# Attention feeding a gated MLP on one core: two heads' float32 scores in the two 64-row halves of the array, v loaded in the order of the keys, and the products of p and v in one group

## The chip, the core and the metric

The kernel runs on 1 core of one Trainium2 chip. The metric is the device time of one execution in microseconds (us). Before the change the median of 3 runs is 748.91 us (748.83 to 749.66).

## What is computed

The reference is rotary attention over 4 batches x 8 heads x 576 positions x 64, and then an MLP with a sigmoid gate over the 2304 resulting rows of 512:

```python
q_rot, k_rot = (rotate(q), rotate(k))
scores = scale * np.matmul(q_rot, k_rot.transpose(0, 1, 3, 2))
scores = scores - np.max(scores, axis=-1, keepdims=True)
attn = np.exp(scores)
attn = attn / (np.sum(attn, axis=-1, keepdims=True) + 1e-09)
attn_out = np.matmul(attn, v)                      # [4, 8, 576, 64]
x = attn_out.transpose(0, 2, 1, 3).reshape(2304, 512)
h = x @ w_in                                       # [2304, 2048]
g = h * (1.0 / (1.0 + np.exp(-1.702 * h)))
out = (g @ w_out).astype(np.float32)               # [2304, 512]
```

## The kernel before

The 32 heads are worked as 16 pairs of heads, pair n from batch n // 4. For each pair `prep` loads q and k, turns them by the rotary angles (three elementwise operations on `RAW` and `BT`, VectorE or GpSimd), transposes them on TensorE (line 455, into `PT`) and copies them out of PSUM. `attention` then makes nine tiles of scores of 128 queries x 576 keys (four per head, and tile 4 with the last 64 queries of both heads), each into one of two PSUM buffers `SPS`. VectorE copies a tile out with its sign turned and finds the extreme of each row (line 602), ScalarE takes the exponential and the sum (line 605), giving `PP` (`PJ` for tile 4). The tiles are transposed on TensorE into `PT`, copied to SBUF, and multiplied with v into `AV`; the result goes to `XS`, is divided by the sums, split into a high and a low part and written to `x_dram`.

There are two ways to full float32 precision. The first pairs use plain float32 matmuls, which TensorE runs in two passes. For the first three pairs (`n_plain_qk=3`) the rotated k and q of one head lie in rows 0 to 63 of a buffer `KP` whose rows 64 to 127 are zero (a GpSimd memset, line 521), one buffer per head, and a score tile is a matmul over all 128 rows, one head at a time (line 585). For the first eight (`n_plain_av=8`) p and v are plain float32 too: `weighted_both` handles the query tiles 0 and 1, then 2 and 3, of both heads, one 128-key step at a time: transpose (line 740) into `PT`, copy into one of two buffers `PW`, and the two heads' matmuls into the two halves of 64 output columns of the array (line 755), with a last matmul over both heads' remaining keys (line 751). `weighted_last` does the same for tile 4 (lines 773 and 789). All other pairs split numbers into a high and a low part in the type fp32r and use more, cheaper matmuls: scores at line 596 from `KA`, `KB`, `QT`, `QZ` (filled by lines 348, 350 and 497, and a DMA that moves 64 rows, line 505), p and v at lines 645 and 673.

The MLP (`moe`) works in 9 chunks of 256 rows of x. For each of 16 column blocks it does 12 matmuls of 256 columns with `win` into `PT` (line 908), a gate (lines 914 and 916, result `T`, split into `G`), and 6 matmuls of 512 columns with `wout` into the second `SPS` buffer (line 925). Its weights are themselves split into high and low parts on the chip (`weight`, lines 858 to 877, buffers `OW`, `CW`, `O`, `CV`). A chunk can start when all pairs of its batch have written their part of `x_dram`; for the fourth pair (n=3) the first 256 rows are written ahead of the rest (`halved0=3`).

The order of all instructions is made when the program is built. Each operation carries a priority (`PLANNED`, `PREP_AT`, `PAIR_AT`, `PAIR_LEN`, `MOE_AT`, `WEIGHT_AT` ...), `Plan.run` plays the operations through once with assumed durations, picks the engine for those that may run on two ("ACT DVE": the first named unless it is later by a wait), and the instructions are issued in the order of the start times that come out. Each engine then works through its own list strictly in order.

## Time and profile before

| | |
|---|---|
| median of the runs | 748.91 us (748.83 to 749.66) |
| span of the profiled execution, first to last instruction | 746.6 us |
| what lies around the span (median less span; the profiled execution's own time is not listed apart) | 2.3 us |
| TensorE (PE) busy | 720.2 us, 96% |
| VectorE (DVE) busy | 496.6 us, 67% |
| ScalarE (ACT) busy | 427.6 us, 57% |
| GpSimd (POOL) busy | 262.1 us, 35% |

Busy time of TensorE is modelled: a float32 matmul shows as two records, one a pass, and each record lasts longer than the distance to the next, because matmuls are pipelined. What a run of matmuls costs is therefore read from the start of its first to the start of what follows. A row of the timeline merges such a run and shows its start, its length, and the number of records.

### The profile page before, as it was taken

The numbers are of one execution on the slowest core, as the hardware profiler recorded it, in microseconds if no ns is written. First come the engines' busy times: TensorE is split into PE (matmuls) and PEld (weight loads), VectorE is DVE, ScalarE is ACT, GpSimd is POOL, SyncE is SP. The second block draws the span as 40 slices with busy tenths as digits, with TensorE's granted clock in tenths as the row PEclk, the third lists the DMA queues.
The fourth block names the chain that finished last, engine by engine and source line by source line (L and its number), as shares of the span: only waits on it lengthen the run. The fifth ranks groups of instructions, "written<-read, shape, count | busy, mean of one in ns | idle before, by whom it ended". The sixth has DMA issues, their size and how long they took to land.

```text
span 746.6 us, 14127 instructions
## 1 busy us (share of the span) xinstructions
PE 720.2 (96%) x4921; PEld 622.3 (83%) x4921; DVE 496.6 (67%) x1188; ACT 427.6 (57%) x1047; POOL 262.1 (35%) x295
## 2 busy tenths in 40 slices
PE   6898979999999999999999999999999999999997
PEld 5565647787777899999999989999999999999896
DVE  5899999788898887467787787877752222322222
ACT  3778778577876764366677666766643232222322
POOL 6566757465554544044343627121110000000000
PEclk8999999999999999999999999999999999999999
DMA  5545477656445653222232343421003020100000
GB/s 133 154 148 129 137 198 196 169 153 178 146 129 159 192 164 104 92 72 60 71 87 74 87 126 102 127 75 35 32 19 115 1 85 0 57 29 1 29 1 29
DMA packets 103911, 72.75 MB, mean 97 GB/s; under 512 B 67856, under 2 KB 88352, under 8 KB 103840
## 3 DMA queue, kind: packets, MB, share of 16 engines
q1 hardware_dynamic: 103840, 71.85, 34.4%
q8 instruction: 39, 0.64, 0.3%
q14 instruction: 32, 0.26, 0.1%
HBM read 48.87 MB, written 15.28 MB: 86 GB/s over the span
## 4 chain that ended last, share of the span: by engine, by line
PE 78%; DVE 11%; ACT 4%; issue 2%; DMA 2%; SPq 1%; POOL 0%; ACTq 0%; DVEq 0%; POOLq 0%
PE PT L908 26%; PE SPS L925 25%; PE SPS L596 8%; PE AV L673 5%; PE PT L645 5%; PE AV L755 3%; PE PT L740 2%; ACT PP L605 1%; DVE PP L602 1%; PE PT L455 1%; DVE RAW L353 1%; DVE QT L497 1%; DMA RAW<-in_q_dram 1%; PE SPS L585 1%; DVE CW L871 1%
## 5 line engine op out<-in xcount | busy, mean ns | idle before, releaser
L908 PE MATMUL PT<-XC,win 128*128 128x256 f32 x1728 | 244.2, 285 | 0.2 <-DVE T L916 0.2
L908 PEld LDWEIGHTS PT<-XC,win 128*128 128x128 f32 x1728 | 227.2, 189 | 11.9 <-DVE T L916 1.5
L925 PE MATMUL SPS<-wout,G 128*128 128x512 f32 x864 | 234.3, 400 | 0.3 <-ACT G L340 0.3
L925 PEld LDWEIGHTS SPS<-wout,G 128*128 128x128 f32 x864 | 150.4, 189 | 25.3 <-issue 0.8
L916 DVE SCALAR_TENSOR_TENSOR T<-T,PT 128x256 f32<-128x256 f32 x144 | 60.2, 418 | 93.2 <-ACT T L914 92.1
L605 ACT ACTIVATE PP<-PP,ST 128x576 f32<-128x576 f32 x128 | 99.3, 776 | 32.2 <-DVE PP L602 31.4
L914 ACT ACTIVATE T<-PT 128x256 f32<-128x256 f32 x144 | 55.1, 383 | 105.4 <-PE PT L908 103.3
L602 DVE TENSOR_SCALAR_CACHE_REDUCE PP<-SPS 128x576 f32<-128x576 f32 x128 | 95.5, 752 | 21.9 <-PE SPS L596 13.9
L353 DVE TENSOR_TENSOR G<-T,G 128x256 fp32r<-128x256 f32 x120 | 54.0, 450 | 62.0 <-ACT G L340 55.0
L340 ACT CAST G<-T 128x256 fp32r<-128x256 f32 x121 | 49.0, 405 | 67.2 <-PE SPS L925 65.4
L344 POOL TENSOR_SCALAR G<-T 128x256 fp32r<-128x256 f32 x23 | 9.6, 417 | 203.7 <-PE SPS L925 149.2
L662 DVE TENSOR_TENSOR PH<-PT,PH 128x512 fp32r<-128x512 f32 (+4 forms) x128 | 65.5, 528 | 18.0 <-ACT PH L340 16.1
L340 ACT CAST PH<-PT 128x384 fp32r<-128x384 f32 (+4 forms) x113 | 49.7, 453 | 36.7 <-PE PT L645 31.0
L673 PE MATMUL AV<-PH,VS 128*128 128x256 f32 (+2 forms) x368 | 60.4, 287 | 0.0
L673 PEld LDWEIGHTS AV<-PH,VS 128*128 128x128 f32 x368 | 53.2, 189 | 2.2 <-DVE PH L662 0.3
L353 POOL TENSOR_TENSOR BT<-RAW,cos_sin_sb 128x512 f32<-128x512 f32 (+1 forms) x35 | 36.6, 1047 | 38.3 <-DMA RAW<-in_k_dram 26.2
L645 PE MATMUL PT<-ident,PP 128*128 128x128 f32 x288 | 47.8, 277 | 0.9 <-DVE PH L662 0.9
L740 PE MATMUL PT<-ident,PP 128*128 128x128 f32 x288 | 44.7, 282 | 3.6 <-ACT PW L340 1.2
L740 PEld LDWEIGHTS PT<-ident,PP 128*128 128x128 f32 x288 | 32.4, 142 | 15.6 <-issue 6.9
L874 POOL TENSOR_TENSOR CV<-CV 128x256 int32<-128x256 int32 x32 | 26.6, 835 | 42.6 <-DVE CV L871 36.8
L755 PE MATMUL AV<-PW,VT 128*64 128x256 f32 x256 | 39.3, 400 | 1.3 <-DVE PW L342 0.9
L340 ACT COPY PW<-PT 128x512 f32<-128x512 f32 (+2 forms) x63 | 31.7, 515 | 14.9 <-PE PT L740 8.6
(113 smaller groups left out, 1037.7 us busy)
## 6 DMA issues: line engine op xcount, KB each, us to landing
XC<-x_dram SPq DMA_DIRECT2D x22, 512.0 KB
x_dram<-XS SPq DMA_DIRECT2D x15, 576.0 KB
out_dram<-O SPq DMA_DIRECT2D x18, 256.0 KB
RAW<-in_q_dram SPq DMA_DIRECT2D x32, 128.0 KB
RAW<-in_k_dram SPq DMA_DIRECT2D x32, 128.0 KB
OW<-in_moe_w_out_dram SPq DMA_DIRECT2D x8, 512.0 KB
OW<-in_moe_w_in_dram SPq DMA_DIRECT2D x8, 512.0 KB
O<-in_moe_w_in_dram SPq DMA_DIRECT2D x16, 256.0 KB
```

Of the source, the lines that this page charges most:

```text
L340: nc.scalar.copy(to, src)
L353: engine[e].tensor_tensor(to, a, b, op=how)
L602: o = vec("DVE", "psum", S, lambda e: nc.vector.tensor_scalar(to().rearrange("p (c s) -> p c s", c=2), s.t[:, :, 0:HALF], -1.0, LARGEST, o ...
L605: return vec("ACT", "sbuf", S, lambda e: nc.scalar.activation(to(), to(), AF.Exp, bias=st.t[:, 0, col:col + 1], scale=-1.0, accum_out=st.t ...
L645: nc.tensor.transpose(pt.t[0:w, to:to + r], p.t[r0:r0 + r, c0:c0 + w], ident[r0:r0 + r, r0:r0 + r])
L662: done.append(vec("DVE", "psum", w, lambda e, src=src, part=part: nc.vector.tensor_tensor(part(1), src(), part(0), op=ALU.subtract), hi, b ...
L673: nc.tensor.matmul(av.t[:, to:to + w], vs[h].t[:, kt].rearrange("p a d -> p (a d)"), ph.t[:, 512 * l + at:512 * l + at + w], start=(first ...
L740: nc.tensor.transpose(pt.t[:, (2 * i + m) * 128:(2 * i + m + 1) * 128], used[m].t[:, c0:c0 + 128], ident)
L755: nc.tensor.matmul(av.t[64 * h:64 * h + 64, 0:256], vt.t[:, 6 * h + kt], pw.t[:, 256 * h:256 * h + 256], start=(kt == 0), stop=False)
L908: nc.tensor.matmul(h.t[:, 0:CT], win[f_i // KH][:, wl, kk, f_i % KH * 128:(f_i % KH + 1) * 128], xc[xl].t[:, kk, :], start=(i == m == 0), ...
L916: o = vec("DVE", "psum", CT, lambda e, h=h, t=t: nc.vector.scalar_tensor_tensor(t.t, t.t, 1.0, h.t[:, 0:CT], op0=ALU.add, op1=ALU.mult), o ...
L925: nc.tensor.matmul(acc.t[:, m, :], g.t[:, a, m * 128:(m + 1) * 128], wout[f_i // KH][:, b, f_i % KH, :], start=(f_i == fs[0] and i == 0), ...
```

## The change

For the first four pairs (three before) q and k are loaded so that the two heads lie beside each other, and a transpose leaves head 0 in rows 0 to 63 and head 1 in rows 64 to 127 of one buffer `KP`. There is nothing to zero. `scores_plain` issues the matmuls of both heads in turn, each over its own 64 rows, into both `SPS` buffers (tile 4: into two halves of one). The keys of both heads now lie in their natural order, so v of the second head is loaded from position 64 on, and its first 64 positions go to the slot of the remainder. Pair 3 moves from the split form to this one.

For pairs 4 to 7 `weighted_plain` makes all transposes and copies of a pair of query tiles first (six `PW` buffers instead of two) and then issues all products as one group; tile 4 is in the second group. The numbers that set the priorities are new throughout, and the early pools have fewer `KA`, `KB`, `QT`, `QZ` and `KP`, and one more `XS` and `PP`. Other new names in the code (`n_direct`, `n_rs`, `n_added`, `n_quarter`) are 0 and do nothing.

```diff
-PLANNED = dict(wait=300.0, wait_dve=300.0, wait_pool=300.0, n_split=2, n_early=4, n_plain_qk=3, n_plain_av=8,
+PLANNED = dict(wait=300.0, wait_dve=300.0, wait_pool=300.0, n_split=2, n_early=4, n_plain_qk=4, n_plain_av=8,
+               n_warm=12, n_direct=0, n_join=4, n_quarter=0, n_added=0, n_rs=0, n_moved=0, halved0=3, halved1=-1,
...
-EARLY = dict(KA=1, KB=1, QT=2, QZ=1, RAW=2, RAW1=1, BT=1, ST=0, XS=0, PP=0, PJ=0, KP=4, OW=2, CW=3)
-MID = dict(PW=2, VT=2)
+EARLY = dict(KA=0, KB=0, QT=0, QZ=0, RAW=2, RAW1=1, BT=1, ST=0, XS=1, PP=1, PJ=0, KP=3, OW=2, CW=3)
+MID = dict(PW=6, VT=2)
...
+        if n in plain_qk:
+            def f():
+                for h in range(2):
+                    if big:
+                        nc.sync.dma_start(raw.t[:, :, h, :],
+                                          (q if s == 0 else k)[b, 2 * j + h, 0:w].rearrange("(t p) d -> p t d", p=128))
...
+        if n in plain_qk:
+            kq = kt_of[n]
+            for l in ((1,), (1, 0), (0,))[s]:
+                c0, wid, to = (0, w, 0) if big else (64 * (1 - l), 64, 512)
+                done.append(vec("ACT DVE" if l == 0 else "DVE ACT", "psum", wid, lambda e, l=l, c0=c0, wid=wid, to=to: scaled(
+                    e, kq.t[:, l, to:to + wid], pt.t[:, c0:c0 + wid], scale if l else 1.0), tr, bufs=[pt, kq], prio=prio))
+            return done
...
-            def f():
-                for kq in kt_of[n]:
-                    nc.gpsimd.memset(kq.t[64:128], 0.0)
...
+                    t0 = 64 if h and not odd else 0
                     nc.sync.dma_start(vt.t[:, 6 * h:6 * h + 4, :],
-                                      v[b, 2 * j + h, 0:512].rearrange("(t p) d -> p t d", p=128))
+                                      v[b, 2 * j + h, t0:t0 + 512].rearrange("(t p) d -> p t d", p=128))
...
+    def scores_plain(n, t, prio, ps):
+        heads = (0, 1)
+        kq, ss = kt_of[n], [plan.buf("SPS")] * 2 if t == 4 else [plan.buf("SPS"), plan.buf("SPS")]
+        def f():
+            for i in range(2):
+                for h in heads:
+                    c = i if t < 4 or not h else 1 - i
+                    rows = slice(64 * h, 64 * h + 64)
+                    for to, k0, w in ([(0, c * HALF, HALF)] if t < 4 or not h else [(0, 64, HALF)] if not c else
+                                      [(0, 64 + HALF, HALF - 64), (HALF - 64, 0, 64)]):
+                        nc.tensor.matmul(ss[h].t[:, c, to:to + w] if t < 4 else ss[h].t[rows, c, to:to + w],
+                                         kq.t[rows, 1, t * 128:t * 128 + (128 if t < 4 else 64)],
+                                         kq.t[rows, 0, k0:k0 + w], start=True, stop=True)
...
+    def weighted_plain(n, t, pb, sp, xs, prio, step, last_at):
+        vt, av = vs_of[n], buf("AV")
...
+        def f():
+            for kt in range(4):
+                for h in range(2):
+                    nc.tensor.matmul(av.t[64 * h:64 * h + 64, 0:256], vt.t[:, 6 * h + kt],
+                                     pws[kt].t[:, 256 * h:256 * h + 256], start=(kt == 0), stop=False)
+            for kt in range(5) if t else ():
+                for h in range(2):
+                    x = pw_last.t[:, kt * 128 + 64 * h:kt * 128 + 64 * h + 64] if kt < 4 else pw4.t[:, 256 + 64 * h:320 + 64 * h]
+                    nc.tensor.matmul(av.t[64 * h:64 * h + 64, 256:320], vt.t[:, 6 * h + kt], x, start=False, stop=False)
+            nc.tensor.matmul(av.t[:, 0:256], vt.t[:, 4:6].rearrange("p a d -> p (a d)"), pw4.t[:, 0:256], start=False,
+                             stop=True)
+        o = pe(f, done, vs_ready[n], f32=[256] * 5 + [64] * (5 if t else 0), beside=5 if t else 4, mode=("half", ""),
+               extra=Plan.DRAIN, bufs=list({id(x): x for x in pws}.values()) + [av, vt], prio=prio + 4 * step + at["prod"])
```

How the instructions move shows best at three places. The first is TensorE at the very start, pair 0: `RAW` holds rotated q and k, `KP_128` and `KP_129` are the buffers of head 0 and head 1 before, and `SPS_66` and `SPS_67` the two score buffers. Before:

```order
L455 MATMUL PT_68<-ident,RAW_72 128x128 x4
L455 MATMUL PT_69<-ident,RAW_74 128x128
L585 MATMUL SPS_66<-KP_128 128x288 x2
L455 MATMUL PT_68<-ident,RAW_73 128x128 x4
L585 MATMUL SPS_67<-KP_128 128x288 x2
L455 MATMUL PT_69<-ident,RAW_124 128x128 x4
L585 MATMUL SPS_66<-KP_128 128x288 x2
L585 MATMUL SPS_67<-KP_129 128x288 x2
```

The same place now (one buffer `KP_129` for both heads):

```order
L475 MATMUL PT_68<-ident,RAW_72 128x128 x4
L475 MATMUL PT_69<-ident,RAW_74 128x128
L475 MATMUL PT_68<-ident,RAW_73 128x128 x4
L627 MATMUL SPS_66<-KP_129 128x288
L627 MATMUL SPS_67<-KP_129 128x288
L627 MATMUL SPS_66<-KP_129 128x288
L627 MATMUL SPS_67<-KP_129 128x288
L627 MATMUL SPS_66<-KP_129 128x288
```

A tile was two matmuls into one buffer; four matmuls now alternate between both buffers, and the first score waits for both transposes of q and k.

The second place is VectorE where q and k of pair 3 leave PSUM, between the copies of score tiles (line 602 before, 646 now). Before, with `KA`, `QT` and so on, the split form:

```order
L350 TENSOR_SCALAR KA_76<-PT_68 64x512
L602 TENSOR_SCALAR PP_99,ST_82<-SPS_66 128x576
L497 SCALAR_TENSOR_TENSOR KA_76<-PT_68,KA_76 64x512
L602 TENSOR_SCALAR PP_99,ST_82<-SPS_67 128x576
L350 TENSOR_SCALAR QT_79<-PT_68 64x512
L602 TENSOR_SCALAR PP_100,ST_82<-SPS_66 128x576
L497 SCALAR_TENSOR_TENSOR QT_79<-PT_68,QT_79 64x512
```

The same stretch of pair 3 now:

```order
L646 TENSOR_SCALAR PP_99,ST_82<-SPS_66 128x576
L646 TENSOR_SCALAR PP_99,ST_82<-SPS_67 128x576
L351 TENSOR_SCALAR KP_131<-PT_68 128x64 x2
L351 TENSOR_SCALAR KP_131<-PT_69 128x512
L646 TENSOR_SCALAR PP_100,ST_82<-SPS_66 128x576
```

The score tiles come in twos, one from each buffer, with other work of VectorE between the twos, and the split of pair 3's q and k is gone.

The third place is TensorE in one of pairs 4 to 7, the product of p (`PW`) and v (`VT`) of its first query tiles, with transposes of p (line 740, `PP`), scores of the next pair (`KA`, `QT`) and MLP matmuls (`win`) around it. Before, two buffers `PW` in turn:

```order
L755 MATMUL AV_71<-PW_112,VT_114 64x256 x2
L755 MATMUL AV_71<-PW_113,VT_114 64x256 x2
L740 MATMUL PT_69<-ident,PP_99 128x128
L740 MATMUL PT_69<-ident,PP_98 128x128
L740 MATMUL PT_69<-ident,PP_99 128x128
L740 MATMUL PT_69<-ident,PP_98 128x128
L755 MATMUL AV_71<-PW_112,VT_114 64x256 x2
L596 MATMUL SPS_66<-KA_76,QT_79 128x288 x4
L755 MATMUL AV_71<-PW_113,VT_114 64x256 x2
L455 MATMUL PT_68<-ident,RAW_73 128x128 x4
```

Such a place now:

```order
L1038 MATMUL PT_70<-XC_88,win_61 128x256 x8
L1038 MATMUL PT_70<-XC_89,win_61 128x256 x4
L607 MATMUL SPS_66<-KA_77,QT_79 128x288 x4
L895 MATMUL AV_71<-PW_112,VT_118 64x256 x2
L895 MATMUL AV_71<-PW_113,VT_118 64x256 x2
L895 MATMUL AV_71<-PW_114,VT_118 64x256 x2
L895 MATMUL AV_71<-PW_115,VT_118 64x256 x2
L901 MATMUL AV_71<-PW_116,VT_118 128x256
```

The products that stood apart, three stretches of them in ten rows, now follow each other, and the whole group stands behind the last copy into a `PW` buffer. Counted over the whole list of TensorE, the stretches of such half-array products that stand behind the first MLP matmul go from 28 to 7.

## Rows read from the trace of the kernel before

**Rows 1.** The page: busy tenths of TensorE, VectorE in 40 equal slices; granted clock.
```profile
PE   6898979999999999999999999999999999999997
DVE  5899999788898887467787787877752222322222
PEclk8999999999999999999999999999999999999999
```

**Rows 2.** Stretches: us; busy PE, PEld, DVE, ACT, POOL (instructions); clock; DMA share; GB/s.
```profile
0.00:128.50 128.50, 110.69 (x712) 76.61 (x713) 110.83 (x251) 91.64 (x202) 82.83 (x82) 0.96 0.58 154
128.50:250.00 121.50, 118.79 (x841) 94.82 (x840) 100.46 (x259) 88.62 (x234) 67.08 (x80) 1.00 0.58 163
250.00:742.30 492.30, 490.76 (x3370) 450.90 (x3368) 285.31 (x682) 246.25 (x611) 112.24 (x135) 1.00 0.23 66
742.30:746.60 4.30, 0.00 (x0) 0.00 (x0) 0.00 (x0) 1.08 (x2) 0.00 (x0) 0.82 0.33 122
```

**Rows 3.** MLP's first matmuls: records, duration min/median/max (ns), first and last start.
```profile
L908 PE MATMUL PT<-XC,win x1728: 274/283/469, 128.5 to 738.7; 128*128 128x256 f32 x192
```

**Rows 4.** VectorE, 0 to 135 us, by form: count, busy us, mean ns, idle before.
```profile
L602 DVE TENSOR_SCALAR_CACHE_REDUCE PP<-SPS 128x576 f32<-128x576 f32 x40 | 29.3, 751 | 4.1 <-PE SPS L585 2.9 <-PE SPS L596 0.7 <-PE PT L740 0.3
L342 DVE COPY PW<-PT 128x512 f32<-128x512 f32 x16 | 10.7, 677 | 1.5 <-PE PT L740 0.9 <-PE AV L755 0.4
L342 DVE COPY KP<-PT 64x512 f32<-64x512 f32 x3 | 2.1, 692 | 0.0
L350 DVE TENSOR_SCALAR KP<-PT 64x64 f32<-64x64 f32 x6 | 1.0, 208 | 0.3 <-PE PT L455 0.3
L497 DVE SCALAR_TENSOR_TENSOR QZ<-PT,QZ 64x64 fp32r<-64x64 f32 x6 | 1.3, 218 | 0.2
L342 DVE COPY XS<-AV 128x256 f32<-128x256 f32 x5 | 2.1, 420 | 0.1
```

**Rows 5.** The chain of waits: start, us, what.
```profile
29.39 1.95 PE SPS L585 x8
...
96.59 3.31 DMA KA<-KA
```

**Rows 6.** Timeline of TensorE, pair 0's scores: start, us, what, records.
```profile
29.23 4.40 PE L585 MATMUL SPS<-KP 128*128 128x288 f32 x22
33.46 0.71 PE L740 MATMUL PT<-ident,PP 128*128 128x128 f32 x5
```

**Rows 7.** Timeline of TensorE: products of p and v, twice and once.
```profile
47.73 1.08 PE L755 MATMUL AV<-PW,VT 128*64 128x256 f32 x8
48.75 0.66 PE L740 MATMUL PT<-ident,PP 128*128 128x128 f32 x4
49.33 0.65 PE L755 MATMUL AV<-PW,VT 128*64 128x256 f32 x4
49.91 0.44 PE L740 MATMUL PT<-ident,PP 128*128 128x128 f32 x2
```

**Rows 8.** Timeline of TensorE, split scores and transposes of p.
```profile
114.49 1.32 PE L596 MATMUL SPS<-KA,QT 128*128 128x288 f32 x8
115.64 0.59 PE L751 MATMUL AV<-PW,VT 128*128 128x256 f32 x2
...
121.58 2.21 PE L740 MATMUL PT<-ident,PP 128*128 128x128 f32 x16
123.72 1.08 PE L755 MATMUL AV<-PW,VT 128*64 128x256 f32 x8
```

**Rows 9.** Timeline of TensorE: a wait ahead of a score tile.
```profile
103.39 0.85 PE L596 MATMUL SPS<-KA,QZ 128*128 128x288 f32 x2 [2.66 <-DVE PP L602]
```

**Rows 10.** Stretches around that wait, columns as in rows 2.
```profile
95.00:100.00 5.00, 3.83 (x26) 1.69 (x24) 4.62 (x10) 4.50 (x9) 1.99 (x2) 1.00 1.06 225
100.00:105.00 5.00, 2.34 (x11) 1.91 (x10) 4.87 (x9) 1.63 (x4) 2.56 (x2) 0.84 0.74 229
105.00:110.00 5.00, 4.31 (x26) 3.21 (x25) 4.27 (x13) 4.96 (x11) 3.78 (x3) 0.82 0.44 135
```

More of the change, by code (lines that the diff above doesn't have):

```diff
@@ L449, in prep_qk @@
                 prio=prio + at["rope"])
-        o = vec(rope, "two", w, lambda e: combine(e, raw.t, raw.t, bt.t[:, 0:n_t], ALU.add), o, bufs=[raw, bt],
-                prio=prio + at["rope"])
+        added = n < at["n_added"]
+        if not added:
+            o = vec(rope, "two", w, lambda e: combine(e, raw.t, raw.t, bt.t[:, 0:n_t], ALU.add), o, bufs=[raw, bt],
+                    prio=prio + at["rope"])
         def f():
-            for i in range(n_t):
-                nc.tensor.transpose(pt.t[:, i * 128:(i + 1) * 128], raw.t[:, i].rearrange("p c d -> p (c d)"), ident)
+            for l, src in enumerate((raw.t, bt.t) if added else (raw.t,)):
+                for i in range(n_t):
+                    nc.tensor.matmul(pt.t[:, i * 128:(i + 1) * 128], src[:, i].rearrange("p c d -> p (c d)"), ident,
+                                     start=(l == i == 0), stop=(i == n_t - 1 and l == added), is_transpose=True,
+                                     skip_group_check=True)
         heads_of = ((0,), (0, 1), (1,))[s]
-        tr = pe(f, o, constants, tr=[128] * n_t, prio=prio + at["turn"], chain=("turn", big),
-                bufs=[raw, pt] + ([] if n in plain_qk else [qt_of[n][s]]) + [kt_of[n][h] for h in heads_of])
+        tr = pe(f, o, constants, tr=[128] * (n_t * (1 + added)), prio=prio + at["turn"], chain=("turn", big),
+                bufs=[raw, pt] + ([bt] if added else []) + ([kt_of[n]] if n in plain_qk else [qt_of[n][s]] + [kt_of[n][h] for h in heads_of]))
         done = []
+        if n in plain_qk:
[5 more added lines that the diff above has]
+            return done
         for h in heads_of:
@@ L578, in f @@
         def f():
-            if n in plain_qk:
-                for c in range(2):
-                    for h, kt in zip(heads, kts):
-                        q0, r = (t % 5 * 128 + 64 * h, 128) if t != 4 else (512 * (1 - h), 64)
-                        r0 = 64 if t == 4 and h else 0
-                        for to, at, w in columns(c, h):
-                            nc.tensor.matmul(s.t[r0:r0 + r, c, to:to + w], kt.t[:, 1, q0:q0 + r],
-                                             kt.t[:, 0, at:at + w], start=True, stop=True)
-                return
             for c in range(2):
@@ L597, in f @@
                                              stop=(i == len(kts) - 1 and l == 1 and to + wid == HALF))
-        work = dict(f32=[HALF] * 2 * len(heads)) if n in plain_qk else dict(mm=[HALF] * 4 * len(heads) + [128] * (2 if t == 4 else 0))
-        mm = pe(f, qt_ready[n][t], *[kt_ready[n][h] for h in heads], **work, bufs=[s] + kts + ([] if n in plain_qk else [qt]), prio=prio)
-        to = lambda: p.t[:, p_at:p_at + S]
+        work = dict(mm=[HALF] * 4 * len(heads) + [128] * (2 if t == 4 else 0))
@@ new lines, in scores @@
+        mm = pe(f, qt_ready[n][t], *[kt_ready[n][h] for h in heads], **work, bufs=[s, qt] + kts, prio=prio)
+        return softened(n, t, s, mm, prio, p, p_at)
+    def scores_plain(n, t, prio, ps):
[11 more added lines that the diff above has]
+                                         kq.t[rows, 0, k0:k0 + w], start=True, stop=True)
+        mm = pe(f, kt_ready[n], f32=[HALF] * 2, beside=2, mode=("rows", "rows"), chain="plain", bufs=[kq] + ss[0:1 if t == 4 else 2], prio=prio)
+        if t == 4:
+            return [softened(n, 4, ss[0], mm, prio, ps[0], 0)]
+        return [softened(n, t + 5 * h, ss[h], mm, prio, ps[h], S * h) for h in heads]
```

162 lines of the change are left out of this document (114 added, 48 removed).

## The prediction

> **What bounds the kernel now.** I read the slices of the page first: TensorE stands at 9 tenths or more from the seventh slice on, with some eights and nines before, while VectorE is at 8 to 9 tenths only through the first part [rows 1]. The first matmul of the MLP says where the one state goes over into the other: it starts at 128.5 us [rows 3]. The table of stretches, cut there, shows two regimes. Up to 128.5 us neither engine is full: TensorE is busy 110.69 us, VectorE 110.83 us, ScalarE 91.64 us. From 128.5 to 742.3 us TensorE is busy 118.79 + 490.76 = 609.6 of 613.8 us [rows 2]: it idles 4.2 us in all. So the time is a sum of two terms: when the first chunk of the MLP can begin (T1, 128.5 us), and how much TensorE work stands behind that point. Work that TensorE loses ahead of T1 is worth only what it moves T1; work that it loses behind T1 counts in full. The last 4.3 us of the span and the 2.3 us around it (748.9 less 746.6) I leave as they are, and set the sum against the median that way.
>
> What sets T1? The chain ahead of it runs mostly over VectorE, ScalarE and the work of pair 3, among it a transfer of 64 rows of `KA` that takes 3.31 us [rows 5]. VectorE's list up to its first MLP instruction, each instruction at the mean of its form in the early stretch, adds up to 121.6 us, TensorE's to about 94 us at the distances of rows 6 to 8, ScalarE's to 99 us. VectorE is the nearest to full, and it waited for plain scores only 2.9 us [rows 4]. I therefore let T1 follow VectorE.
>
> **Part 1, VectorE ahead of T1.** The list now holds, ahead of the first MLP instruction:
> - copies of q and k into `KP`: before six of 64x512 (692 ns) and ten of 64x64 (some 210 ns), 6 x 0.69 + 10 x 0.21 = 6.2 us. Now six of 128x512 and five of 128x64. No row has these; the nearest with the same columns are the `PW` copy of 128x512, 677 ns, and the 64x64 form, 208 ns [rows 4]: 6 x 0.68 + 5 x 0.21 = 5.1 us. A gain of 1.1 us.
> - eight 64x64 splits of `KA`, `KB`, `QZ` fewer at 0.22 us: 1.8 us. The wide splits are as many as before, because those of pairs 4 and 5 come ahead of T1.
> - four copies `XS<-AV` fewer at 0.42 us, two casts fewer: 2.7 us with one multiplication more.
> - three wide `PW` copies more at 0.68 us and two narrow ones: 2.6 us lost.
> - rope and weights: 0.5 us lost.
>
> Sum: 2.5 us less, and ScalarE loses about 3 us. On GpSimd six memsets of `KP` give way to six small ones of `PW`. T1 becomes 126.1 us (I take 2.4). The two transfers that pair 3 no longer makes for its keys also leave the chain; I cost that at nothing, since VectorE's list covers it.
>
> **Part 2, TensorE ahead of T1.** Two tiles of plain scores cost 1.95 us, 0.975 each [rows 5]. No row shows two halves of 64 rows at work; the nearest are the two halves of 64 columns: a group of four records takes 0.44 us more when it follows another (1.02 for two, from 47.73 to 48.75, against 0.58 for one, from 49.33 to 49.91) [rows 7], what one 256-column product alone would take, so they run side by side. With rows alike, two heads' tiles cost 0.975 instead of 1.95. Tile 4 used column halves already: 4.23 us for the 22 records less three tiles leave 1.3 us [rows 6]. Per pair this is 4 x 0.975 = 3.9 us less, less a change of mode for each of four groups, 0.14 (below): 3.3 us, 10 us for pairs 0 to 2. Pair 3 cost 1.15 us for two split tiles [rows 8], 4 x 1.15 + 1.3 = 5.9 us, and now 4 x 1.1 + 1.3 = 5.7: nothing. Bounds for the halves: 10 us less, or, one after the other, 4 x 3.9 - 9.9 = some 6 us more with pair 3 and the changes of mode. Ahead of T1 I count neither, as TensorE has 17.8 us free there [rows 2].
>
> The Trainium skill (TensorE: Matmul & The Clock Gate, Part 3, "Measured speedup vs the span model") gives 3.07 for four row tiles, not 4. As an estimate at that share two halves would give 1.54, and the gain of pairs 0 to 2 would be half of what I work out; no run here shows it yet, and the sum by it is the same.
>
> **Part 3, TensorE behind T1.** Entering and leaving the half mode costs 0.58 - 0.44 = 0.14 us [rows 7]. Behind the first MLP matmul such stretches go from 28 to 7: 21 x 0.14 = 2.9 us less. Sixteen transposes of p and four of q and k stand ahead of T1 now that stood behind it; at 2.14 us for sixteen (121.58 to 123.72) [rows 8], 0.134 each, that is 2.7 us. All other kinds of matmul are as many as before on that side. Together 5.6 us, which counts in full as long as TensorE stays as full as the 4.2 us of idle time say. The grouping adds a wait: each of the eight groups stands behind its last `PW` copy, with all of TensorE's later work queued behind it. MLP matmuls stand ahead of the groups and cover a copy of 0.68 us [rows 4]; uncovered, it costs 8 x 0.68 = 5.4 us.
>
> **Sum.** 748.9 - 2.4 - 5.6 = 740.9 us (span 738.6).
>
> **Rivals.**
> - *T1 follows TensorE.* If TensorE's own list is what paces the early stretch (its 110.69 us are as many as VectorE's [rows 2]), T1 falls by the whole 10 us: 748.9 - 10 - 5.6 = 733.3 us. Against it: VectorE waits for plain scores 2.9 us only [rows 4].
> - *The row halves run one after the other.* TensorE has 6 us more ahead of T1. T1 lies between 2.4 us earlier (hidden in the free 17.8 us) and 6 us later; halfway, 1.9 later: 748.9 + 1.9 - 5.6 = 745.2 us. For it: only column halves are shown side by side.
> - *Slower: both score buffers are taken at once.* A group of both heads needs both `SPS` buffers empty, so VectorE finds no tile while TensorE makes the next two. Where nothing else is queued on VectorE, each of the 20 groups costs it 0.975 us. Eight such groups eat the gain; with 15 it is 748.9 - 8 + 15 = 755.9 us. Idle TensorE pays again: behind the wait of 2.66 us [rows 9] the granted clock is 0.84 and 0.82 for ten microseconds [rows 10], that is stretches at 1.2 GHz instead of 2.4. Against it: in VectorE's list other work stands between nearly all twos of tiles. The Trainium skill (TensorE: Matmul & The Clock Gate, Part 1) states that the engine is throttled by default and activity releases it; this trace agrees with its 0.84 after the wait.
> - *The groups wait for their copies*, uncovered as above: 740.9 + 5.4 = 746.3 us.
>
> **How the numbers follow.** This kernel's runs cannot tell less than 0.2%, 1.5 us, from no change. Chances: the sum 0.56 (its own range 735 to 746, as T1 may move by 3 us and the idle time behind it by 2), T1 with TensorE 0.15, halves in turn 0.10, both buffers taken 0.12, uncovered groups 0.07. Faster (below 747.4): 0.55 + 0.15 + 0.07 + 0.03 = 0.80. Slower (above 750.4): nearly all of the 0.12 and a little of the others, 0.13. The rest, 0.07, is the same. The range for 8 in 10 leaves out most of the slower rival and the lower tail of the first: 733 to 750 us.
>
> **What would show it.** In the trace after: two heads' tiles (eight records) in about 1 us show the halves side by side, 1.95 us that they are not. The first MLP matmul near 126 us shows part 1 right; near 118 the first rival, behind 129 the second or third. VectorE's waits for plain scores above some 8 us, or more stretches with a clock of 0.8 ahead of T1, speak for the third. A group of products should run through in one piece, its predecessor ending without a gap; TensorE's idle time behind T1 should stay near 4 us. I am wrong if that idle time grows beyond 8 us, if T1 moves later, or if the group's records show no saving.

## The result and the profile after

The changed kernel takes 741.63 us (median of 4 runs, 741.17 to 742.49) against 749.03 us for the kernel before on the same chip; the ratio is 0.9903, with a 95% interval from 0.9889 to 0.9917. The forecast was 740.9 us. As the sections below show, the two terms of its sum are off in opposite directions, so that its nearness to the result is in part luck.

The page, as [rows 1]: busy tenths of TensorE and VectorE in 40 slices, and the granted clock.

```profile
PE   6899797999999999999999999999999999999997
DVE  5999999888889886477788788788752222222322
PEclk7999998999999999999999999999999999999999
```

VectorE is a little fuller than before in the early slices, TensorE is not, and the clock is lower in the first and in the seventh slice. The first matmul of the MLP starts 3.8 us earlier than in [rows 3], the last one 6.3 us earlier:

```profile
L1038 PE MATMUL PT<-XC,win x1728: 274/283/562, 124.7 to 732.4; 128*128 128x256 f32 x192
```

The stretches, cut at that matmul as in [rows 2] and with the same columns (us; busy TensorE, its weight loads, VectorE, ScalarE, GpSimd, with the numbers of instructions; granted clock; DMA share; GB/s):

```profile
0.00:124.70 124.70, 103.64 (x734) 70.40 (x734) 110.49 (x239) 88.03 (x204) 84.18 (x86) 0.95 0.59 160
124.70:250.00 125.30, 119.23 (x875) 102.45 (x874) 107.20 (x261) 88.60 (x231) 65.86 (x81) 0.97 0.54 158
250.00:736.00 486.00, 484.13 (x3317) 445.10 (x3315) 283.71 (x671) 243.41 (x603) 104.06 (x130) 1.00 0.23 66
736.00:740.30 4.30, 0.00 (x0) 0.00 (x0) 0.00 (x0) 1.08 (x2) 0.00 (x0) 1.00 0.33 122
```

Ahead of T1 TensorE is busy 7 us less (103.64 against 110.69) and VectorE as long as before (110.49 against 110.83), in a stretch that is 3.8 us shorter. Behind T1 TensorE idles 611.3 - 603.4 = 7.9 us; it was 4.2. The clock of 0.97 in the second stretch is new, too.

Two places show the edits at work. In the timeline of TensorE (start, us, what, records), two heads' tiles of plain scores in pair 0, to be held against [rows 5]:

```profile
29.59 1.24 PE L627 MATMUL SPS<-KP 64*128 64x288 f32 x8
30.76 1.52 PE L819 MATMUL AV<-PW,VT 128*64 128x256 f32 x12
```

From the first start to the next it is 1.17 us for eight records; before, it was 1.95 us. Not every group runs like that. Of the sixteen, ten take 1.17 to 1.35 us; the first two, at half clock, take 6.03 us together; and four take 1.84 us, among them this one (TensorE, then VectorE's copy that frees the second score buffer):

```profile
86.43 1.91 PE L627 MATMUL SPS<-KP 64*128 64x288 f32 x8 [2.27 <-DVE PP L646]
86.30 0.75 DVE L646 TENSOR_SCALAR_CACHE_REDUCE PP<-SPS 128x576 f32<-128x576 f32 x1
```

The group starts when the first of the two buffers is free, and the second head's records start 0.68 us behind the first's, when that copy has ended. And in the timeline just ahead of the MLP, a group of products of p and v:

```profile
117.24 0.66 PE L882 MATMUL PT<-ident,PP 128*128 128x128 f32 x4 [0.74 <-DVE PW L343]
117.82 1.95 PE L895 MATMUL AV<-PW,VT 128*64 128x256 f32 x16
119.70 0.70 PE L901 MATMUL AV<-PW,VT 128*128 128x256 f32 x2
121.44 0.63 PE L475 MATMUL PT<-ident,RAW 128*128 128x128 f32 x4 [1.04 <-ACT PW L341]
123.92 1.11 PE L882 MATMUL PT<-ident,PP 128*128 128x128 f32 x4 [1.85 <-DVE QZ L519]
124.69 2.05 PE L1038 MATMUL PT<-XC,win 128*128 128x256 f32 x8
```

The group lasts 1.88 us from its start to the next, four times the 0.44 of a pair of products in [rows 7] and 0.12 once; there is no idle time ahead of it. But the two rows behind it say what is new: TensorE waits 1.04 us for a copy of ScalarE and 1.85 us for the split of a q (`QZ`) on VectorE, and the MLP's first eight records then last 2.05 us. The granted clock there, by stretches of 5 us (columns as above, the clock is the third number from the end):

```profile
115.00:120.00 5.00, 3.75 (x26) 2.33 (x27) 4.94 (x12) 3.25 (x11) 2.29 (x3) 1.00 0.71 181
120.00:125.00 5.00, 2.10 (x11) 1.50 (x10) 4.83 (x9) 2.56 (x5) 3.58 (x3) 0.82 0.78 226
125.00:130.00 5.00, 5.00 (x25) 4.67 (x24) 4.28 (x7) 2.61 (x7) 1.28 (x1) 0.50 0.65 164
130.00:135.00 5.00, 5.00 (x37) 4.73 (x37) 3.15 (x9) 2.83 (x8) 3.51 (x4) 1.00 0.94 291
```

TensorE was busy 2.10 of the 5 us ahead of 125; from 125 to 130 it is full, but at a granted clock of 0.50, that is at 1.2 GHz. The kernel before went over into its MLP (at 128.5 us) at a clock of 1.00:

```profile
125.00:130.00 5.00, 5.00 (x40) 4.08 (x38) 4.31 (x10) 4.66 (x14) 4.70 (x4) 1.00 1.09 330
```

A second fall lies further on, from 167.5 to 171.0 us, behind waits of TensorE of 1.04 and 1.61 us. The 0.97 of the second stretch is made of both.

```profile
165.00:170.00 5.00, 2.43 (x12) 2.23 (x13) 4.76 (x11) 3.81 (x11) 3.17 (x6) 0.75 0.59 152
170.00:175.00 5.00, 5.00 (x35) 4.12 (x36) 3.68 (x11) 2.61 (x8) 1.09 (x2) 0.90 0.26 63
```

### The profile page after: what moved, and what is told of

Its sections match the earlier page's. It is cut to its first block, busy times and chain, and to the rows that moved or that the text cites. A ratio compares the mean times of both kernels' runs of the same rounds, so it can differ in the third digit from the quotient of the medians.

```text
span 740.3 us, 14104 instructions
## 1 busy us (share of the span) xinstructions
PE 707.0 (95%) x4921; PEld 618.0 (83%) x4921; DVE 501.4 (68%) x1168; ACT 421.1 (57%) x1038; POOL 254.1 (34%) x297
## 4 chain that ended last, share of the span: by engine, by line
PE 80%; DVE 9%; ACT 4%; DMA 3%; issue 2%; POOL 1%; SPq 1%; ACTq 0%; DVEq 0%; POOLq 0%
PE PT L1038 26%; PE SPS L1055 25%; PE SPS L607 8%; PE AV L737 5%; PE PT L709 5%; PE SPS L627 2%; PE PT L882 2%; PE PT L804 1%; PE AV L895 1%; PE PT L475 1%; DVE PP L646 1%; PE AV L819 1%; DMA RAW<-in_k_dram 1%; ACT PP L649 1%; DVE RAW L354 1%
## 5 line engine op out<-in xcount | busy, mean ns | idle before, releaser
L646 DVE TENSOR_SCALAR_CACHE_REDUCE PP<-SPS 128x576 f32<-128x576 f32 x128 | 94.9, 750 | 21.1 <-PE SPS L607 16.5
L341 ACT CAST G<-T 128x256 fp32r<-128x256 f32 x115 | 46.6, 405 | 64.4 <-PE SPS L1055 61.2
L345 POOL TENSOR_SCALAR G<-T 128x256 fp32r<-128x256 f32 x29 | 11.9, 412 | 203.7 <-PE SPS L1055 154.9
L726 DVE TENSOR_TENSOR PH<-PT,PH 128x512 fp32r<-128x512 f32 (+4 forms) x128 | 65.7, 528 | 19.3 <-ACT PH L341 17.4
L341 ACT CAST PH<-PT 128x512 fp32r<-128x512 f32 (+4 forms) x115 | 50.9, 457 | 33.8 <-PE PT L709 29.3
L737 PE MATMUL AV<-PH,VS 128*128 128x256 f32 (+2 forms) x368 | 62.4, 289 | 0.0
L354 POOL TENSOR_TENSOR BT<-RAW,cos_sin_sb 128x512 f32<-128x512 f32 (+1 forms) x33 | 32.8, 994 | 46.2 <-DMA RAW<-in_k_dram 42.4
L709 PE MATMUL PT<-ident,PP 128*128 128x128 f32 x288 | 48.2, 277 | 0.1
L354 POOL TENSOR_TENSOR RAW<-RAW,BT 128x512 f32<-128x512 f32 (+1 forms) x36 | 36.2, 1006 | 12.5 <-DVE RAW L354 8.3
L607 PE MATMUL SPS<-KB,QT 128*128 128x288 f32 x192 | 35.9, 308 | 0.9 <-DVE PJ L646 0.8
L341 ACT COPY PW<-PT 128x512 f32<-128x512 f32 (+2 forms) x59 | 29.4, 516 | 11.7 <-PE PT L882 9.0
```

Of the source, the lines that this page charges most:

```text
L341: nc.scalar.copy(to, src)
L354: engine[e].tensor_tensor(to, a, b, op=how)
L607: nc.tensor.matmul(s.t[:, c, to:to + wid], w, kt.t[:, l, at:at + wid], start=(i == l == 0), stop=(i == len(kts) - 1 and l == 1 and to + wi ...
L646: o = vec("DVE", "psum", S, lambda e: nc.vector.tensor_scalar(to().rearrange("p (c s) -> p c s", c=2), s.t[:, :, 0:HALF], -1.0, LARGEST, o ...
L709: nc.tensor.transpose(pt.t[0:w, to:to + r], p.t[r0:r0 + r, c0:c0 + w], ident[r0:r0 + r, r0:r0 + r])
L726: done.append(vec("DVE", "psum", w, lambda e, src=src, part=part: nc.vector.tensor_tensor(part(1), src(), part(0), op=ALU.subtract), hi, b ...
```

## Experiments

Each edit is made to the changed kernel, where nothing else is said. T1 is the start of the first MLP matmul, TL that of the last. The chips differ from run to run, so a time is to be read by its ratio to the kernel before on the same chip. T1 lies between 124.0 and 126.0 us in the six profiles that do the changed kernel's work ahead of it in full (after, after_again, heads_in_turn and the three filled ones, which add only some matmuls without use); a difference of 2 us in T1 is therefore little.

| run | time, us | ratio to before [95%] | T1 | TL - T1 | TensorE idle ahead of / behind T1 |
|---|---|---|---|---|---|
| before | 749.03 | 1 | 128.5 | 610.1 | 17.8 / 4.2 |
| after | 741.63 | 0.9903 [0.9889, 0.9917] | 124.7 | 607.7 | 21.1 / 7.9 |
| after_again | 740.65 | 0.9874 [0.9857, 0.9891] | 125.6 | 607.4 | 20.6 / 8.7 |
| scores_twice | 752.26 | 1.0037 [1.0019, 1.0055] | 136.0 | 608.1 | 13.1 / 9.7 |
| kp_copies_twice | 743.63 | 0.9915 [0.9892, 0.9938] | 128.8 | 604.4 | 19.0 / 8.0 |
| one_half | 753.50 | 1.0053 [1.0032, 1.0075] | 138.1 | 605.6 | 13.3 / 8.9 |
| heads_in_turn | 741.52 | 0.9900 [0.9886, 0.9915] | 126.0 | 605.5 | 16.6 / 8.7 |
| before_grouped | 761.12 | 1.0159 [1.0131, 1.0187] | 127.7 | 623.3 | 18.3 / 17.8 |
| no_group | 751.32 | 1.0025 [1.0013, 1.0038] | 126.7 | 615.1 | 16.0 / 11.6 |
| pair3_split | 762.04 | 1.0178 [1.0146, 1.0211] | 137.7 | 613.0 | 29.7 / 13.7 |
| filled_late | 740.93 | 0.9879 [0.9858, 0.9901] | 124.0 | 604.6 | 14.8 / 8.4 |
| filled_late_again | 740.08 | 0.9877 [0.9860, 0.9895] | 125.4 | 604.4 | 15.1 / 8.1 |
| filled_both | 742.28 | 0.9901 [0.9884, 0.9918] | 125.5 | 608.3 | 13.5 / 9.8 |
| narrow_add | 737.33 | 0.9848 [0.9821, 0.9875] | 118.9 | 606.9 | 13.9 / 8.7 |

### Which engine's work moves T1

More work for TensorE: each plain score is made twice.

```diff
-            for i in range(2):
+            for i in (0, 1, 0, 1):
```

> The changed kernel with the matmuls of every plain score group of pairs 0 to 3 issued twice (the second time writes the same values over the first): 20 groups x 0.97 us = some 19.5 us more TensorE work ahead of the MLP's first matmul, 124.7 us, where TensorE stands idle 21 us; VectorE's list is as it was. Theory 1 (VectorE paces the stretch ahead of the MLP): most of it is hidden, the first MLP matmul comes 0 to 6 us later, time 741.6 to 748 us. Rival (TensorE's own list paces it): the first MLP matmul comes about 19 us later, time about 760 us.

T1 went from 124.7 to 136.0 us. TensorE's busy time ahead of T1 grew by 19.2 us (103.6 to 122.9); 11.3 came through, 0.59 of it, and 7.9 went into its idle time. Against the second profile of the changed kernel it is 10.4 of 17.8, as large a share. More work for VectorE: its copies of q and k into `KP` are made twice.

```diff
...
-                    e, kq.t[:, l, to:to + wid], pt.t[:, c0:c0 + wid], scale if l else 1.0), tr, bufs=[pt, kq], prio=prio))
+                    e, kq.t[:, l, to:to + wid], pt.t[:, c0:c0 + wid], scale if l else 1.0) for _ in range(2 if e == DVE else 1)],
+                    tr, bufs=[pt, kq], prio=prio))
```

> The changed kernel with VectorE's nine copies of q and k of the first pairs out of PSUM made twice (8 of 128 columns wide tiles, 512 or 64 columns): by the planned split 6 x 0.69 + some 5 x 0.21 us = about 5 us more on VectorE ahead of the MLP, nothing on TensorE. Theory 1 (VectorE paces): first MLP matmul about 5 us later, near 129.5 us, time about 746.5 us. Rival (TensorE or a chain of latencies paces): less than 2 us, 741.6 to 743.5 us.

Some 5.1 us more for VectorE (six copies of 0.68 us and five of 0.21) moved T1 by 4.1 us, or 3.2 against the second profile. The ratio to before (0.9915 against 0.9903) doesn't show it, because the half clock now lay ahead of T1 (121.6 to 125.0 us) and TL - T1 was 3.3 us shorter. So VectorE's work counts by 0.6 to 0.8, as far as one profile tells; and TensorE's counts by some 0.6, which the prediction had at nothing.

### Do the row halves run side by side?

Both heads read the same half of the rows, so that the second head's own scores are left out; sizes, counts, buffers and waits stay.

```diff
+                    src = rows if t == 4 else slice(0, 64)
...
-                                         kq.t[rows, 1, t * 128:t * 128 + (128 if t < 4 else 64)],
+                                         kq.t[src, 1, t * 128:t * 128 + (128 if t < 4 else 64)],
...
```

> The changed kernel, but in the plain scores of tiles 0 to 3 both heads read rows 0 to 63 of KP (the second head's scores are then those of the first; the count, sizes, buffers and waits of all instructions stay). Theory: two heads cost 1.17 us because their matmuls lie on different halves of the rows and run side by side. On one half they run one after the other: a group of eight records takes about 1.95 us, 0.8 us more, 16 groups 12 to 14 us more TensorE work ahead of the MLP. By the run with doubled scores (19.5 us more work moved the first MLP matmul by 11.3) the first MLP matmul then starts 6 to 8 us later, near 131 to 133 us, and the time is 746 to 750 us. Rival: a 64-row matmul is cheap by itself, wherever it lies: the groups stay at 1.17 us and the time at 741.6 us within 1.5.

The timeline of TensorE in this run, the tile pair that took 1.17 us above:

```profile
32.52 2.21 PE L628 MATMUL SPS<-KP 64*128 64x288 f32 x8
34.65 1.51 PE L820 MATMUL AV<-PW,VT 128*64 128x256 f32 x12
```

It is 2.13 us: on one half they run one after the other. Sixteen groups by 0.96 us are 15.4 us more work, and T1 moved by 12.5 to 13.4 us (from 125.6 and 124.7), more than the 6 to 8 expected. That is not another share than above: TensorE's busy time ahead of T1 grew by 19.8 and 21.2 us, as the granted clock was at half for 34 us there, against 22 and 12 in the two profiles of the changed kernel; 0.63 of it came through both times. The other way to lose the overlap would be the order of issue: all of head 0 first, then head 1.

```diff
-            for i in range(2):
-                for h in heads:
+            for h in heads:
+                for i in range(2):
```

> The changed kernel with the matmuls of the two heads of a plain score group one head after the other instead of in turn: the same matmuls, but only the last of head 0 and the first of head 1 can lie side by side. A group of eight records takes about 1.46 to 1.95 us instead of 0.97, that is 8 to 19 us more TensorE work ahead of the MLP. From the doubled scores (19.5 us more work moved the MLP's first matmul by 11.3 us): theory 1b (TensorE and VectorE pace that stretch together, some 0.6 us for each us of TensorE work) gives a first MLP matmul 5 us later, near 129.5 us, time about 746 us. Rival (only what exceeds the idle time counts): less than 2 us later.

The time stayed, and so did the group, in the timeline of this run:

```profile
29.44 1.25 PE L627 MATMUL SPS<-KP 64*128 64x288 f32 x8
30.61 1.51 PE L819 MATMUL AV<-PW,VT 128*64 128x256 f32 x12
```

1.17 us again. The expectation that the heads would then follow each other is wrong: the single records start in twos, 0.013 us apart (0.007 when issued in turn), though two matmuls of one head were issued ahead of the other's. (A record doesn't name its half; this is read from the spacing and from the length of the group.)

### The parts one by one

The grouped products alone, put into the kernel before with its own priorities (with `weighted_plain` as in the change):

```diff
-               n_warm=12, n_moved=0, halved0=3, halved1=-1, half0=0.454, n_wide_s=5, n_wide_t=6, split0=4.733,
+               n_warm=12, n_join=4, n_moved=0, halved0=3, halved1=-1, half0=0.454, n_wide_s=5, n_wide_t=6, split0=4.733,
...
-MID = dict(PW=2, VT=2)
+MID = dict(PW=6, VT=2)
```

> The kernel before with one part of the change alone: the products of p and v of pairs 4 to 7 in one group (six PW buffers), all priorities as they were. Stretches of half-array products behind the MLP's first matmul go from 28 to 7. Theory (a stretch costs 0.14 us to enter and leave): 21 x 0.14 = 2.9 us less from the first to the last MLP matmul (610.2 us in the kernel before), the first one near 128.5 us, time 745 to 746.5 us. Rival A (a stretch costs more, since the missing 4 us of TensorE work behind the MLP's start must come from somewhere): 5 to 7 us less. Rival B (the groups wait for their copies): no gain, or slower by up to 5 us.

The changed kernel without the grouping, and with pair 3 in the split form, each with the new priorities:

```diff
-               n_warm=12, n_direct=0, n_join=4, n_quarter=0, n_added=0, n_rs=0, n_moved=0, halved0=3, halved1=-1,
+               n_warm=12, n_direct=0, n_join=8, n_quarter=0, n_added=0, n_rs=0, n_moved=0, halved0=3, halved1=-1,
```

> The changed kernel with the products of pairs 4 to 7 as before (one 128-key step at a time, 27 stretches behind the MLP's first matmul instead of 7), all else and all priorities as changed; the planner places the rest anew. Theory (0.14 us a stretch): 20 x 0.14 = 2.8 us more behind the MLP's start, time about 744.5 us. Rival A (a stretch costs more): 4 to 7 us more, 746 to 749 us. Rival B (the groups' wait for copies eats their gain): no more than 1 us.

```diff
-PLANNED = dict(wait=300.0, wait_dve=300.0, wait_pool=300.0, n_split=2, n_early=4, n_plain_qk=4, n_plain_av=8,
+PLANNED = dict(wait=300.0, wait_dve=300.0, wait_pool=300.0, n_split=2, n_early=4, n_plain_qk=3, n_plain_av=8,
```

> The changed kernel with pair 3's scores in the split form as before (n_plain_qk=3), so that only pairs 0 to 2 use the halves; the planner places the rest anew. VectorE gets back some 3 us of split work and pair 3 its 3.3 us transfer of keys, TensorE the same work (5.9 against 5.7 us). Theory 1 (VectorE paces): first MLP matmul 2 to 4 us later, time 744 to 746 us. Rival (pair 3's form is worth nothing by itself, the gain is that of pairs 0 to 2 on TensorE): within 1 us of the changed kernel.

All three are slower than both kernels, the second only a little slower than the kernel before (1.0025). In the first, the products behind T1 fell from 19.3 to 15.5 us as they should, but TensorE waits; these are its largest waits behind T1 (engine, line, waited for: us in all, times, longest):

```profile
PE SPS L602 <- DVE PP L608: 4.2, 6, 1.6
PE PT L968 <- DVE T L976: 2.9, 2, 1.9
PE PT L824 <- DVE QZ L503: 2.7, 3, 1.2
```

All three lie 7 to 18 us above what was expected of them. That an order made for another set of instructions costs so much, more than the change gains, is the likely reason, but it isn't shown by itself; pair3_split besides has fewer buffers for pair 3 than the kernel before, as the early pools of `KA`, `KB`, `QT` and `QZ` are now empty. So these runs don't price the parts: that remains to the sums from the trace below. How much of the gain the new priorities brought, apart from the edits, stays open.

### The half clock at the start of the MLP

Matmuls of no use are put in TensorE's queue just ahead of the MLP, into a corner of a score buffer that is free there; one variant also puts 14 at the start.

```diff
+        extra = {id(on_pe[i + first if i < 0 else i]): n for i, n in ((-1, 8), (-2, 4), (-4, 3))}
+        for o in todo:
+            for _ in range(extra.get(id(o), 0)):
+                nc.tensor.matmul(plan.tiles["SPS"][0][:, 0, 320:448], plan.tiles["T"][0][:, 0:128],
+                                 plan.tiles["T"][0][:, 0:128], start=True, stop=True)
```

> The changed kernel with 15 matmuls of zeros (float32, 128 columns, written to columns that nothing reads) put on TensorE ahead of three waits in the last 8 us before the MLP: 3, 4 and 8 of them. In the changed kernel the granted clock stands at 0.50 from 123.2 to 130 us, after waits of 1.04 and 1.85 us, so that the first 5.3 us of the MLP run at 1.2 GHz. Theory 2 (the clock ate the part of the gain behind the MLP's start that is missing): the clock stays at 1.00, the first MLP matmul stays at 124.7 to 125.2 us, time 2 to 3 us less, about 739 us. Rival (the missing part is waits of TensorE behind the MLP's start, 7 us in sum against 4): clock mended and time within 1 us of 741.6.

> As filled_late, and 14 more such matmuls ahead of the wait of 3.6 us at 8.4 us, behind which the clock of the changed kernel stands at 0.50 from about 10 to 20 us and VectorE waits 2.0 us for the first scores. Theory 1 (VectorE paces): the first scores come 1 to 2 us sooner, VectorE's wait for them shrinks by as much, and the MLP starts 1 to 1.5 us sooner, time about 1 us below filled_late, 738 us. Rival (what follows is paced by transfers and GpSimd): no difference to filled_late.

> The changed kernel with 15 matmuls of no use ahead of the first MLP matmul, once more, now beside the changed kernel on the same chip. Theory: the half clock in the MLP's first 5 us costs about 3 us and the fill takes it away: the first MLP matmul near 124 us, from there to the last one 604 to 606 us, granted clock 1.00 from 115 to 145 us, the time 2 to 4 us below the changed kernel's beside it. Rival: the fill only moves the half clock or the waits elsewhere: no difference within 1 us.

> The changed kernel as it is, for the comparison with the filled one. Both theories: 741 to 742.5 us. If the half clock at the start of the MLP belongs to the order of the instructions, it shows again between 123 and 130 us; if it is chance of one execution, it stands elsewhere or is gone.

The stretches of the first filled run, columns as above:

```profile
120.00:125.00 5.00, 4.78 (x41) 4.41 (x40) 4.83 (x9) 3.32 (x7) 3.22 (x3) 1.00 0.78 226
125.00:130.00 5.00, 3.36 (x26) 2.87 (x24) 4.46 (x9) 1.89 (x6) 1.31 (x2) 1.00 0.72 189
```

The clock stays at 1.00, and TL - T1 is 604.6 and 604.4 us in the two profiles of filled_late against 607.7 and 607.4 in the two of the changed kernel. Only the second pair prices the start of the MLP alone, 3.0 us with 0.6 of idle time in it, since the 607.7 also hold the fall at 167.5 us. The changed kernel showed 0.88 and 0.50 in the same two stretches when it ran again, so the half clock there is not chance. But little moves it: in kp_copies_twice and heads_in_turn, without any fill, it lay just ahead of T1.

The other profiles of this order bear the price out. No half clock lies behind T1 in kp_copies_twice, one_half, heads_in_turn and the two of filled_late: TL - T1 is 604.4 to 605.7 us. In after, after_again, scores_twice, narrow_add and filled_both some does: 606.9 to 608.3 us. In the last three it stands between 162 and 184 us; filled_both, whose MLP starts at 1.00, has its half clock from 169.1 to 172.6 us and 9.8 us of idle time, so its 608.3 don't speak against the price.

In the medians the gain of filled_late is 0.7 and 0.6 us, within the intervals; the expected 2 to 4 us did not show. The clocks of all executions say why, in part: their mean is 0.980 in the changed kernel, both times, and 0.983 and 0.982 in filled_late (0.989 to 0.998 in the kernel before). One stretch of 6.8 us, at full clock instead of half, would have raised the mean by 0.005, so not every execution gained all of it. The fill at the start brought the mean to 0.987, with less half clock ahead of 26 us (10.2 us instead of 17.1 in filled_late), and no gain in time.

### What lengthens VectorE's work

GpSimd's addition in the preparation of the early weights is cut from 512 columns to 32 or 8.

```diff
...
-                a().bitcast(I32), a().bitcast(I32), r(), op=ALU.add), o, low, bufs=[cv], prio=prio)
+                a().bitcast(I32)[:, :, 0:w], a().bitcast(I32)[:, :, 0:w], r()[:, :, 0:w], op=ALU.add), o, low, bufs=[cv], prio=prio)
```

> The changed kernel, with GpSimd's addition in the preparation of the early weights (16 instructions of 128x512, 1.54 us each, ahead of the MLP) cut to 8 columns of 128; the low bits of those weights are left out, the order and number of all instructions stay. Theory: VectorE's list ahead of the MLP did not get shorter, because its instructions on SBUF last 1.2 to 1.8 us instead of 0.3 to 0.7 where a GpSimd instruction runs beside them; in the changed kernel's trace some 13 us of VectorE's time ahead of the MLP are such lengthening, 3.8 of them beside this addition. With it cut, VectorE's instructions ahead of its first of the MLP add up to 3 to 5 us less than 128.6, and the first MLP matmul starts 1 to 4 us earlier (121 to 124 us); time 737 to 741 us. Rival: the long instructions have another cause (transfers, their own operands): VectorE's sum stays within 1 us of 128.6, and the first MLP matmul within 1 us of 125.

T1 is 118.9 us, 5.8 earlier and more than expected, and the time 737.33 us. The two forms that suffered most, in the changed kernel and in this run (us up to the first MLP instruction of VectorE; count, busy us, mean ns):

```profile
L996 DVE TENSOR_SCALAR CW<-CW 128x512 f32<-128x512 f32 x16 | 9.7, 625 | 0.6 <-ACT CW L994 0.6
L354 DVE TENSOR_TENSOR BT<-RAW,cos_sin_sb 128x512 f32<-128x512 f32 x6 | 6.3, 1045 | 5.1 <-DMA RAW<-in_q_dram 3.6 <-issue 1.4
```

```profile
L996 DVE TENSOR_SCALAR CW<-CW 128x512 f32<-128x512 f32 x16 | 8.8, 571 | 2.3 <-ACT CW L994 2.3
L354 DVE TENSOR_TENSOR BT<-RAW,cos_sin_sb 128x512 f32<-128x512 f32 x6 | 4.1, 687 | 4.2 <-DMA RAW<-in_q_dram 3.7 <-DVE RAW L354 0.4
```

Neither form was touched. `BT` came from 1045 to 687 ns because its neighbours on GpSimd moved: the one that starts 0.29 us behind a GpSimd instruction in the changed kernel lasts 1.76 us, and here, where it starts 0.09 us ahead of the same one, 0.68 us. Summed over all instructions ahead of VectorE's first of the MLP, the durations fell from 128.6 to 122.4 us. GpSimd's own busy time fell, too, from 85.5 to 69.1 us up to there, so that T1 could have gained from a shorter GpSimd list; VectorE's idle time did not shrink (14.4 and 15.3 us), which speaks for the durations, but no run separates the two. This kernel leaves the low bits of those weights out, so it is not one to use, and moving the addition elsewhere would be worth at most what it shows.

## Why the prediction was right, and where it was not

**T1: near the number, but not by the term.** The step by which VectorE's list is 2.5 us shorter was to bring T1 to 126.1 us; it came to 124.7 (125.6 in the second profile). Counted at the durations of before, the list up to VectorE's first MLP instruction did become shorter, by 3.5 us. But durations did not stay. In the trace of before, over the same part of the program:

```profile
L866 DVE TENSOR_SCALAR CW<-CW 128x512 f32<-128x512 f32 x16 | 7.8, 503 | 1.0 <-ACT CW L864 0.9
L353 DVE TENSOR_TENSOR BT<-RAW,cos_sin_sb 128x512 f32<-128x512 f32 x3 | 2.1, 697 | 3.6 <-DMA RAW<-in_k_dram 3.6
```

Held against 625 and 1045 ns, and over all forms, that is 5.6 us more, so that the sum of durations went from 126.5 to 128.6 us. (Instructions that follow each other overlap in the trace: VectorE's busy time up to there is 113.2 us before and 114.0 after.) What lengthens them is seen in the timelines of VectorE and GpSimd in the changed kernel, side by side:

```profile
53.63 1.44 DVE L996 TENSOR_SCALAR CW<-CW 128x512 f32<-128x512 f32 x1
```

```profile
53.51 1.27 POOL L354 TENSOR_TENSOR RAW<-RAW,BT 128x512 f32<-128x512 f32 x1
```

The shortest of these VectorE instructions takes 386 ns; this one starts 0.12 us behind a GpSimd instruction and ends 0.29 us behind it: 1.15 us of overlap and then some 0.3 us of its own. All 17 instructions from SBUF to SBUF that last over a quarter longer than the shortest of their form lie beside a GpSimd instruction, 13.8 us of lengthening in all (9.6 before), and narrow_add took 6.2 us of duration away by cutting GpSimd's part alone. The Trainium skill (SBUF — State Buffer, "Who interferes with whom") says that VectorE and GpSimd share a pair of ports which one of them holds for a whole instruction while the other waits; these rows agree, and the prediction should have weighed it, since moving rope and weights between the engines is what a new order does.

That T1 still fell is due to VectorE's idle time, which I had let stand: it went from 18.3 to 14.4 us up to that first MLP instruction. That this came near the 2.4 us of the forecast is luck. The largest waits of VectorE there, before:

```profile
DVE BT L353 <- DMA RAW<-in_k_dram: 3.6, 1, 3.6
DVE PP L602 <- PE SPS L585: 2.9, 6, 1.0
DVE RAW L353 <- POOL BT L353: 1.8, 2, 0.9
DVE PW L342 <- ACT PW L340: 1.0, 1, 1.0
```

and after:

```profile
DVE BT L354 <- DMA RAW<-in_q_dram: 3.6, 1, 3.6
DVE PP L646 <- PE SPS L627: 2.4, 2, 2.0
DVE BT L354 <- issue: 1.4, 1, 1.4
DVE PW L343 <- PE PT L804: 1.1, 3, 0.5
```

The first two stayed; the waits for GpSimd and ScalarE are gone from the top. Which edit or which priority removed them is not separated, so the cause of the earlier T1 stays open that far.

**TensorE ahead of T1.** The 0.975 us for two heads' tiles and 0.14 for a change of mode give 1.11; 1.17 was measured, with 2.13 when both heads lie on one half. That TensorE's gain counts as nothing ahead of T1 is only half right. TensorE's busy time ahead of T1 fell by 7 us, T1 by 3.8, and its idle time grew from 17.8 to 21.1 us: so about half of the saving did turn into idle time. And added work comes through by some 0.6 (0.59 in scores_twice, 0.63 in one_half). At that share TensorE's 7.1 us alone would account for all of the 3.8; no run shows that they do. Two engines that hand buffers to each other both pace the stretch; free time summed over it is not cover at each place. The estimate of 1.54 for the gain of two halves is too low here: it is 2.13 / 1.17 = 1.82. Nor would 1.54 have halved the 3.3 us a pair, as the prediction says; 4 x (1.95 - 1.27 - 0.14) leaves 2.2.

**TensorE behind T1.** The two terms of the sum came out about as forecast. Read from starts to next starts, from T1 to the end of TensorE's work, in us:

| kind | before | after | filled_late | predicted change |
|---|---|---|---|---|
| products of p and v, half and full array | 21.4 | 18.4 | 18.4 | -2.9 |
| transposes of p, q and k | 57.8 | 54.4 | 53.6 | -2.7 |
| MLP matmuls, both layers | 420.0 | 420.2 | 417.7 | 0 |
| idle time | 4.2 | 7.9 | 8.4 | 0 |
| TL - T1 | 610.1 | 607.7 | 604.6 | -5.6 |

All other kinds differ by less than 0.5 us between before and after. The transposes hold a surplus: the twenty that moved ahead of T1 account for 1.8 us (the forecast had 2.7), and the 60 of tile 4, as many as before, take 1.6 us less. The MLP's matmuls take 2.5 us less when the clock is held, and are then 2.3 us below before, where the clock was 1.00. Some 1 us of that is a price of the half mode that 0.14 left out: an MLP record just ahead of such a stretch lasts some 0.09 us longer than one ahead of another of its kind, and there are 14 of them before, 4 after. The rest is not explained.

So what failed is the step "counts in full as long as TensorE stays as full". TensorE idles 3.7 us more, and the two stretches at half clock add some 3 us, which the prediction had at nothing; 2.3 us less of MLP work and the shorter transposes make up for part of it. In the profiles without half clock behind T1, TL - T1 is 4.4 to 5.7 us shorter than before, close to the 5.6, in spite of 8 to 9 us of idle time. The new idle time is, behind T1 in the changed kernel:

```profile
PE PT L882 <- DVE QT L519: 1.7, 2, 1.3
PE PT L684 <- DVE PW L343: 1.6, 1, 1.6
PE PT L882 <- DVE QZ L519: 1.6, 2, 1.0
PE SPS L607 <- DVE PJ L646: 0.8, 2, 0.6
```

against, before:

```profile
PE PT L645 <- DVE PH L662: 0.9, 3, 0.3
PE PT L620 <- DVE ST L617: 0.6, 1, 0.6
```

Transposes of p queue behind the split of the next pair's q on VectorE, and one of the sums (`ST`) behind a copy; the groups of products themselves have no part in it:

```profile
L895 PE MATMUL AV<-PW,VT 128*64 128x256 f32 x128 | 15.6, 385 | 0.0
```

So -3.8 instead of -2.4 ahead of T1 and -2.4 instead of -5.6 behind it; what lies behind TL moved by nothing (7.9 and 8.0 us). The span fell by 6.3 us in the profiled execution, which took 742.06 us, 0.4 more than the median. What lies around a span is 1.7 to 1.8 us in every run that lists both, not the 2.3 of the sum: held against the span (738.6 forecast, 740.3 measured) the forecast is 1.7 us off, against the median 0.7. The prediction's own limit for TensorE's idle time behind T1, 8 us, was just kept in the one profile (7.9) and passed in the other (8.7).

**The rivals.** T1 with TensorE: T1 did not come to 118, but the probes give TensorE a share that I had denied it. Halves in turn: excluded, by 1.17 against 2.13 us. Both buffers taken at once: VectorE's waits for plain scores are 2.4 us for `PP` and 0.8 for `PJ`, far below the 8 from which it would speak. But its mechanism is there in small: four groups wait inside for their second buffer, 0.67 us each, and the clock fell behind a wait for score buffers as well, in the second profile of the changed kernel (half clock from 86.2 to 93.1 us), where the group shown above at 1.84 us takes 2.89:

```profile
86.84 2.96 PE L627 MATMUL SPS<-KP 64*128 64x288 f32 x8 [2.28 <-DVE PP L646]
```

In the kernel before, the fall that the prediction read as ten microseconds stood from 103.4 to 106.8 us; its two rows share it.

Uncovered groups: no idle time ahead of any of the 128 records.

## What to carry to other kernels

Sum an engine's list with the durations that its neighbours leave it: in this kernel an instruction of VectorE from SBUF to SBUF lasts up to three times as long and more beside one of GpSimd that started before it, and a new order changes which lie beside each other. Where two engines pass buffers to and fro, work on either moves the end, and what idle time is worth as cover has to be probed by adding work on one engine at a time. When a stretch at full load begins just behind a wait, look at its clock first, and look for every other fall before you price one of them; and don't price one edit by undoing it under an order that was made for all of them.
